# A chained accumulator read once at its third link, with the difference taken from SBUF

## Chip, cores and metric

One of the eight cores of a Trainium2 chip (trn2) runs the kernel. The metric is the device time of one execution in microseconds. The kernel before took 1004.42 us in the median of three runs (1003.59, 1004.42, 1004.70).

## What is computed

A gated recurrence over 6080 steps, two sequences, 256 channels, and then a feed-forward layer with 2048 hidden units and ELU. In float32:

```python
sig = 1.0 / (1.0 + np.exp(-f_logit))
f = lower_bound + (1.0 - lower_bound) * sig
for t in range(S):
    h = f[:, t] * h + (1.0 - f[:, t]) * x[:, t]
    y[:, t] = h
h = y.reshape(B * S, D) @ w_in
g = np.where(h > 0.0, h, np.exp(np.minimum(h, 0.0)) - 1.0)
out = g @ w_out
```

## The kernel before

Channels lie on the 128 partitions (two halves), time on the free axis. The sequence is cut into 12 pieces of 512 columns (one of 448); in each piece the 2048 hidden units are done in 8 steps ("quads", `quad`, line 924) of 2 x 128 units for both sequences. A quad multiplies the piece of y by a block of w_in (names M1 to M7, seven products in place of eight, after Strassen's scheme, into PSUM banks `hx`, `hv`, `hz`), applies ELU on ScalarE and VectorE (`elu`, tiles `e`, `g`, `hs`), splits the result into a rounded high part `gh` and a rest `gl` (`split`), and multiplies by a block of w_out, adding into four PSUM accumulators `o00`, `o01`, `o10`, `o11` (`second`, matmuls on line 797). Every product is made of three matmuls: high by high, high by low, low by high.

The work around the change: from the fourth piece on (number 3, counted from 0) the first quad of each piece is "wide": its second product too is done with seven products instead of eight. Four of them, P1, P6, P7 and P5 in this order (`wide_product`, line 838), go one after another into the same accumulator, `o11`, a chain: each link's running total is also a share of another output. So between the links `o11` is read out into the output tiles in SBUF (`out_tile`, traced as `v`): after P1 and P6 by ScalarE (k1, k2), after P7 twice: by ScalarE (k3, the copy of line 419, into the first sequence's output) and by VectorE (k4, subtracted from the second sequence's output); after P5 by VectorE again (k5, added to the same output). k4 and k5 both run through the helper of line 408 and read `v<-v,o`. There are nine wide quads, so nine of each. P5 may write `o11` only when every reader of the third link is done, and k3 and k4, which read the same bank, stand one after the other too.

The order of work on each engine is written by a planner before the program is built: `Plan.add` records every operation with an engine, a cost, a wanted time and what it reads and writes; `Plan.order` (line 223) simulates the engines with these costs and sorts all operations by the start it found; a table of shifts (`SHIFT`) moves single ones. Each engine then works through its own list in order, waiting on semaphores where an operation needs another engine's result.

Behind k5 on VectorE come, according to the piece, `q<-q,hz` (a sum over the bank `hz`, line 408), after which M2 may add into `hz`, or `g<-hv,e` (the ELU's last step, line 750), after which M7 may add into `hv`. Both M2 and M7 are matmuls of line 710.

Of the kernel before, what the change touches and what calls it, by code (L numbers as in the profile page):

```python
# [11 lines left out]
ALU = mybir.AluOpType  # L12
# [139 lines left out]
def wide(q):  # L152

    return q >= WIDE_FROM * MP and place(q)[1] < WIDE


def place(q):

    p, j = divmod(q, MP)
    return p, SECOND[j] if p == 1 else j  # L160


class Plan:
# [22 lines left out]

    def add(
        self, eng, cost, want, fn, reads=(), writes=(), adds=(), takes=(), lock=False, soonest=0.0,
        latest=None, other=None,
    ):  # L190

        i = len(self.ops)
        key = f"{self.key}.{self.count}"
        self.count += 1
        deps = set()
        for b in reads:
            w, r, a = self.last.setdefault(b, [set(), set(), set()])
            deps |= w | a  # L200
            r.add(i)
        for b in adds:
            w, r, a = self.last.setdefault(b, [set(), set(), set()])
            if r:
                self.last[b] = [set(), set(), {i}]
                deps |= w | r | a
                self.last[b][0] = set(w | r | a)
            else:
                deps |= w
                a.add(i)  # L210
        for b in writes:
            w, r, a = self.last.setdefault(b, [set(), set(), set()])
            deps |= w | r | a
            self.last[b] = [{i}, set(), set()]
        deps.discard(i)
        used = set(reads) | set(writes) | set(adds)
        self.ops.append(dict(
            eng=eng, cost=cost, want=want + SHIFT.get(key, 0.0), fn=fn, key=key, deps=deps, used=used, takes=list(takes),
            lock=lock, soonest=max(soonest + SHIFT.get(key + "@", 0.0), self.gate),
            latest=latest, other=other, patience=self.PATIENCE + SHIFT.get(key + "~", 0.0),  # L220
        ))

    def order(self):
        ops = self.ops
        n = len(ops)
# [40 lines left out]
        dropped = set()  # L266
        start = [0.0] * n
        done = [0.0] * n
        left = n
        while left:  # L270
            best = None
            for e, mine in waiting.items():
# [8 lines left out]
                for i in mine:  # L281
                    o = ops[i]
# [18 lines left out]
            t, _, i, _, e = best  # L301
            o = ops[i]
# [30 lines left out]
                        waiting[x].add(j)  # L333
        self.start, self.done = start, done
        assert not left
        return sorted(set(range(n)) - dropped, key=lambda i: (start[i], i))


def act_cost(n, ptr=False):
# [3 lines left out]
def dve_cost(n, fast=False):  # L343
    return 0.15 + n / (1920 if fast else 960)
# [11 lines left out]
def kernel(  # L356
# [7 lines left out]
    nc = tc.nc  # L364
# [8 lines left out]
    plan = Plan({**sizes, "h": 4, **{o: 1 for o in ("o00", "o01", "o10", "o11")}})  # L373
# [15 lines left out]
    def tl(kind, name, shape, dtype=F32):  # L389

        if name not in T:
            T[name] = pool[kind].tile(shape, dtype, tag=kind, name=kind)
        return T[name]
# [20 lines left out]
    def act(n, want, out_, in_, func=ACTF.Copy, ptr=None, **kw):  # L414
        args = {k: kw.pop(k) for k in ("scale", "bias") if k in kw}

        def fn():
            if func == ACTF.Copy:
                nc.scalar.copy(out=out_(), in_=in_())  # L419
            elif ptr:  # L420
                nc.scalar.activation(
                    out=out_(), in_=in_(), func=func, scale=ptr[0], bias=ptr[1]
                )
            else:
                nc.scalar.activation(out=out_(), in_=in_(), func=func, **args)  # L425

        plan.add("ACT", act_cost(n, ptr is not None), want, fn, **kw)
# [239 lines left out]
    def size(q):  # L667
        return SIZES[q // MP]
# [188 lines left out]
    def out_tile(p, t):  # L857
        return tl("v", ("out", p, t), [P, KD, SIZES[p]])

    def keep(p, e, t, want, op=None):  # L860

        o = ("out", p, t)
        reads = [("acc", p, 1, 1), o]
        if op is None:
            act(SIZES[p], want, lambda: out_tile(p, t)[:, e], lambda: accs[p, 1, 1],
                reads=reads, writes=[(o, e)], takes=[("v", o)])
        else:
            tt("DVE", SIZES[p], want, lambda: out_tile(p, t)[:, e], lambda: out_tile(p, t)[:, e],
               lambda: accs[p, 1, 1], op, psum=True, reads=reads, writes=[(o, e)],
               takes=[("v", o)])  # L870
# [53 lines left out]
    def quad(q):  # L924
        p, i = place(q)
        n = size(q)
        b = base(q)
        tail = q == NQ - 1
        w = wide(q)
        o = lambda name, value: plan.at(f"{stage(p)}{q % MP}.{name}", b + value)  # L930
        product = lambda name, bk, start, off: products(
            q, bk, [(LEFT[name], name)], start, o(name, off - 20))
        product("M1", "x", True, 0.0)
        product("M3", "v", True, 0.7)
        product("M4", "z", True, 1.4)
        qn = ("q", q)
        act(n, o("q", 0.9), lambda: tl("q", qn, [P, n]), lambda: hb(q, "x"), reads=[bank(q, "x")],
            writes=[qn], takes=[("q", qn)])
        for bk, off in (("v", 1.5), ("z", 2.2)):
            tt("DVE", n, o("q" + bk, off), lambda: T[qn], lambda: T[qn], lambda bk=bk: hb(q, bk),  # L940
               ALU.add, psum=True, reads=[bank(q, bk)], writes=[qn])
        product("M5", "v", False, 2.9)
        product("M2", "z", False, 4.8)
        g = ("g", q, 1)
        g1 = dict(name=g, tiles=[(1, 0), (0, 1)], pool="raw" if w else "g1", slots=4 if w else 2)
        elu(q, g1, 1, lambda: hb(q, "v"), [bank(q, "v")], o("e1", 3.7), True)
        elu(q, g1, 0, lambda: hb(q, "z"), [bank(q, "z")], o("e0", 5.6), True)
        product("M7", "v", False, 6.8)
        product("M6", "z", False, 8.8)
        if w:  # L950
            split(q, g, "DVE", o("s1", 8.2), (0,), ("b21", q))
            wide_product(q, 0, 0, 4 + 2, ("b21", q), 0, o("P2", 11))
        else:
            split(q, g, "DVE", o("s1", 8.2))
            second(q, g1, o("L1", 11))
        hs = ("hs", q)
        for j, (bk, off) in enumerate((("v", 7.6), ("z", 9.8))):
            tt("DVE", n, o("h" + bk, off), lambda j=j: tl("hs", hs, [P, 2, n])[:, j],
               lambda: T[qn], lambda bk=bk: hb(q, bk), ALU.subtract, psum=True,
               reads=[qn, bank(q, bk), hs], writes=[(hs, j)], takes=[("hs", hs)])  # L960
        g2 = dict(name=hs, tiles=[(0, 0), (1, 1)], pool="hs")
        elu(q, g2, None, lambda: T[hs].rearrange("p c n -> p (c n)"), [(hs, 0), (hs, 1)],
            o("e2", 10.9), False)
        if not w:
            split(q, hs, "DVE" if tail else "POOL", o("s2", 15))
            second(q, g2, o("L2", 18))
            return
        split(q, hs, "DVE", o("s2", 13))
        x, y = ("x", q), ("y", q)

        def xt():
            return T[g][:, 2:4]

        T_x = lambda: T.setdefault(x, xt())
        tt("DVE", 2 * n, o("X", 13.2), T_x, lambda: T[g][:, 1:2].to_broadcast([P, 2, n]),
           lambda: T[hs], ALU.subtract, reads=[g, (g, 1), hs, (hs, 0), (hs, 1)],
           writes=[(x, 0), (x, 1)])
        split(q, x, "DVE", o("sX", 14), hold=[g])
        tt("DVE", n, o("Y1", 15), lambda: T[hs][:, 1], lambda: T[hs][:, 1], lambda: xt()[:, 0],
           ALU.subtract, either=True, reads=[hs, g, (x, 0)], writes=[(hs, 1)])  # L980
        tt("DVE", n, o("Y0", 15.5), lambda: T[hs][:, 0], lambda: T[g][:, 0], lambda: T[hs][:, 1],
           ALU.subtract, either=True, reads=[g, (g, 0), hs, (hs, 1)], writes=[(hs, 0)])
        held = split(q, hs, "DVE", o("sY", 16), (0, 1), y, raw=YRAW)
        wide_product(q, 1, 1, 4 + 0, hs, 0, o("P1", 16))
        keep(p, 0, 0, o("k1", 17))
        wide_product(q, 0, 1, 2, hs, 1, o("P3", 17))
        wide_product(q, 1, 1, 1, y, 1, o("P6", 19), held)
        keep(p, 0, 1, o("k2", 20))
        wide_product(q, 1, 1, 3, x, 1, o("P7", 20))
        keep(p, 1, 0, o("k3", 21))  # L990
        keep(p, 0, 1, o("k4", 21), ALU.subtract)
        wide_product(q, 1, 1, 0, x, 0, o("P5", 21))
        keep(p, 0, 1, o("k5", 22), ALU.add)
        wide_product(q, 1, 0, 4 + 3, y, 0, o("P4", 21), held)
# [24 lines left out]
    for dst, a, b in ((fb, -0.5, 0.5), (fa, 0.5, 0.5)):  # L1019
# [3 lines left out]
                out=dst, in0=lb_sb, scalar1=a, scalar2=b, op0=ALU.mult, op1=ALU.add  # L1023
# [36 lines left out]
    for p in range(NP):  # L1060
        st = stage(p)
        if p:
# [5 lines left out]
            late = p > WIDE_FROM  # L1068
# [84 lines left out]
```

## Time and profile before

| | |
|---|---|
| median of three runs | 1004.42 us (1003.59 to 1004.70) |
| the profiled execution's own time | 1003.18 us |
| its span, first to last instruction | 1001.1 us |
| TensorE matmuls busy | 989.8 us (99%), 4338 |
| TensorE weight loads busy | 812.5 us (81%) |
| ScalarE busy | 806.9 us (81%) |
| VectorE busy | 786.5 us (79%) |
| GpSimd busy | 539.0 us (54%) |
| mean granted clock of TensorE | 0.998 |
| chain that ended last | 95% TensorE, 3% VectorE, 1% ScalarE |

PE stands for TensorE's matmuls, PEld for its weight loads (one ahead of each matmul, beside the matmul in front of it), DVE for VectorE, ACT for ScalarE, POOL for GpSimd. Busy matmuls overlap, so 99% doesn't mean that none can be late; a load that starts late is the sign of it.

### The profile page before, as it was taken

The page shows a single profiled execution, that of the slowest core. Times are in us where ns is not written, and L with a number is a line of the kernel's source. Part 1 is how long each engine was busy: PE and PEld are TensorE (multiplying, and loading weights), DVE is VectorE, ACT ScalarE, POOL GpSimd, SP SyncE. Part 2 cuts the span into 40 slices and gives each one's busy share as a digit, 9 for nine tenths or more (in the row PEclk, how much of TensorE's full clock was granted, in tenths as well). Part 3 has the DMA queues.
Part 4 walks back from the last instruction along what each step waited for, and adds up shares of the span by engine and source line. Part 5 has one row for each costly group of instructions (what it writes and reads, how often), then busy time and mean ns, then how long its engine had stood idle before and what let it go on. Part 6 is the DMA issues. An engine that isn't in the chain of part 4 may idle for free.

```text
span 1001.1 us, 11968 instructions
## 1 busy us (share of the span) xinstructions
PE 989.8 (99%) x4338; PEld 812.5 (81%) x4338; DVE 786.5 (79%) x958; ACT 806.9 (81%) x1137; POOL 539.0 (54%) x303
## 2 busy tenths in 40 slices
PE   7999999999999999999999999999999999999998
PEld 4788899888888878888888888888888888888886
DVE  7889788898888798778678678768767867877655
ACT  6888888977788789789788778888878978877864
POOL 0343647545548537654753862763765475376531
PEclk9999999999999999999999999999999999999999
DMA  5331202000030030021012003003002101200101
GB/s 210 127 121 37 97 31 84 36 1 1 1 127 1 1 126 1 1 85 43 1 53 74 1 1 127 1 1 127 1 0 84 43 1 49 78 1 0 43 1 43
DMA packets 9707, 46.51 MB, mean 46 GB/s; under 512 B 1200, under 2 KB 1200, under 8 KB 7088
## 3 DMA queue, kind: packets, MB, share of 16 engines
q1 hardware_dynamic: 9504, 45.75, 12.8%
q8 instruction: 34, 0.56, 0.2%
q14 instruction: 25, 0.20, 0.1%
q10 hardware_dynamic: 144, 0.00, 0.0%
HBM read 33.29 MB, written 12.45 MB: 46 GB/s over the span
## 4 chain that ended last, share of the span: by engine, by line
PE 95%; DVE 3%; ACT 1%; DMA 0%; issue 0%; DVEq 0%; ACTq 0%
PE o L797 50%; PE hz L710 17%; PE hv L710 17%; PE hx L710 6%; DVE y L638 1%; DMA raw<-w 0%; DVE v L408 0%; DVE gl L408 0%; PE h(_181 L695 0%; ACT e L425 0%; DVE e L750 0%; DVE raw L629 0%; DVE wiL L408 0%; DVE hs L750 0%; PE h(_267 L710 0%
## 5 line engine op out<-in xcount | busy, mean ns | idle before, releaser
L408 POOL TENSOR_TENSOR gl<-hs,gh 128x1024 fp32r<-128x1024 f32 (+1 forms) x79 | 199.2, 2526 | 195.3 <-ACT gh L419 187.6
L425 ACT ACTIVATE e<-e 128x512 f32<-128x512 f32 (+3 forms) x278 | 208.4, 757 | 6.6
L797 PE MATMUL o<-gh,woL 128*128 128x512 f32 (+1 forms) x706 | 212.5, 387 | 0.0
L797 PE MATMUL o<-gh,woH 128*128 128x512 f32 (+1 forms) x706 | 211.2, 387 | 0.1
L797 PE MATMUL o<-gl,woH 128*128 128x512 f32 (+1 forms) x706 | 208.6, 387 | 0.1
L710 PE MATMUL hz<-yo,wiH 128*128 128x512 f32 (+1 forms) x504 | 194.4, 390 | 0.3 <-DVE g L750 0.3
L710 PE MATMUL hv<-yo,wiH 128*128 128x512 f32 (+1 forms) x504 | 192.6, 388 | 0.0
L797 PEld LDWEIGHTS o<-gl,woH 128*128 128x128 f32 x706 | 132.4, 188 | 27.0 <-DVE gl L408 0.8
L797 PEld LDWEIGHTS o<-gh,woH 128*128 128x128 f32 x706 | 132.5, 188 | 26.8 <-ACT v L419 0.5
L797 PEld LDWEIGHTS o<-gh,woL 128*128 128x128 f32 x706 | 132.5, 188 | 26.4 <-ACT gh L419 0.2
L750 DVE SCALAR_TENSOR_TENSOR hs<-hs,e 128x1024 f32<-128x1024 f32 (+1 forms) x84 | 123.6, 1472 | 30.6 <-ACT e L425 30.5
L408 POOL TENSOR_TENSOR ys<-y 128x512 f32<-128x512 f32 (+1 forms) x52 | 95.0, 1830 | 70.8 <-DVE y L638 70.8
L419 ACT CAST gh<-hs 128x1024 fp32r<-128x1024 f32 (+1 forms) x95 | 98.7, 1039 | 35.2 <-PE o L797 17.2
L710 PEld LDWEIGHTS hz<-yo,wiH 128*128 128x128 f32 x504 | 94.6, 188 | 22.4 <-DVE q L408 2.3
L710 PEld LDWEIGHTS hv<-yo,wiH 128*128 128x128 f32 x504 | 94.6, 188 | 20.1 <-DVE g L750 0.2
L425 ACT ACTIVATE e<-hs 128x1024 f32<-128x1024 f32 (+1 forms) x84 | 88.3, 1051 | 26.6 <-DVE hs L408 19.6
L710 PE MATMUL hz<-yo,wiL 128*128 128x512 f32 (+1 forms) x252 | 97.9, 388 | 0.0
L710 PE MATMUL hv<-yo,wiL 128*128 128x512 f32 (+1 forms) x252 | 97.9, 388 | 0.0
L419 ACT CAST gh<-g 128x1024 fp32r<-128x1024 f32 (+1 forms) x80 | 83.1, 1039 | 15.0 <-PE o L797 10.0
L425 ACT ACTIVATE e<-hv 128x512 f32<-128x512 f32 (+1 forms) x84 | 49.8, 593 | 47.3 <-PE hv L710 29.4
L408 DVE TENSOR_TENSOR gl<-g,gh 128x1024 fp32r<-128x1024 f32 (+1 forms) x57 | 75.7, 1328 | 14.5 <-PE o L797 8.0
L408 POOL TENSOR_TENSOR gl<-g,gh 128x1024 fp32r<-128x1024 f32 (+1 forms) x23 | 57.4, 2496 | 54.6 <-PE o L797 36.3
(379 smaller groups left out, 1657.4 us busy)
## 6 DMA issues: line engine op xcount, KB each, us to landing
raw<-fx SPq DMA_DIRECT2D x20, 1024.0 KB, 4.9
out_t<-v SPq DMA_DIRECT2D x22, 512.0 KB, 2.7
raw<-w SPq DMA_DIRECT2D x16, 512.0 KB, 4.7
raw<-fx SPq DMA_DIRECT2D x2, 896.0 KB, 4.6
gh<-fx SPq DMA_DIRECT2D x2, 512.0 KB, 6.1
gl<-fx SPq DMA_DIRECT2D x2, 512.0 KB, 6.9
out_t<-v SPq DMA_DIRECT2D x2, 448.0 KB, 3.5
lb_sb<-lb ACTq DMA_DIRECT2D x1, 1.0 KB, 4.2
```

Of the source, the lines that this page charges most:

```text
L408: return e, cost, lambda: engines[e].tensor_tensor(out=out_(), in0=in0(), in1=in1(), op=op)
L419: nc.scalar.copy(out=out_(), in_=in_())
L425: nc.scalar.activation(out=out_(), in_=in_(), func=func, **args)
L638: nc.vector.tensor_tensor_scan(out=y4[:, a, :n], data0=f([k])[:, 0], data1=x([k])[:, 0], initial=init, op0=ALU.mult, op1=ALU.subtract,)
L710: nc.tensor.matmul(out=hb(q, b), lhsT=(wiH if m == "h" else wiL)[:, i, wi], rhs=T[kind, p, name], start=(start and j == 0), stop=(j == len ...
L750: lambda: nc.vector.scalar_tensor_tensor(out=gt(), in0=src(), scalar=0.0, in1=et(), op0=ALU.max, op1=ALU.subtract,), reads=src_names + [e] ...
L797: nc.tensor.matmul(out=accs[p, e, t], lhsT=lhsT, rhs=rhs, start=(c == 1), stop=(c == total(p, e, t)), skip_group_check=True,)
```

## The change

k4 no longer reads the accumulator. It subtracts k3's copy, which lies in SBUF (the first sequence's output tile), from the second sequence's output. In the planner it is recorded at the same place, with the same cost and the same reads as before, so that everything else is planned as it was; a new mark, `late`, then lifts it out of the finished list and puts it right behind the next VectorE operation that depends on it, which is k5. So the output first gets k5's sum and then the difference.

```diff
     def add(
         self, eng, cost, want, fn, reads=(), writes=(), adds=(), takes=(), lock=False, soonest=0.0,
-        latest=None, other=None,
+        latest=None, other=None, late=False,
     ):
...
         self.start, self.done = start, done
         assert not left
-        return sorted(set(range(n)) - dropped, key=lambda i: (start[i], i))
+        line = sorted(set(range(n)) - dropped, key=lambda i: (start[i], i))
+
+        for i in [i for i in line if ops[i]["late"]]:
+            k = next(k for k in range(line.index(i) + 1, len(line))
+                     if i in ops[line[k]]["deps"] and ops[line[k]]["eng"] == ops[i]["eng"])
+            line.insert(k, line.pop(line.index(i)))
+        return line
...
         keep(p, 1, 0, o("k3", 21))
-        keep(p, 0, 1, o("k4", 21), ALU.subtract)
+        o0, o1 = ("out", p, 0), ("out", p, 1)
+        plan.add(
+            "DVE", dve_cost(n), o("k4", 21), lambda: nc.vector.tensor_tensor(
+                out=out_tile(p, 1)[:, 0], in0=out_tile(p, 1)[:, 0], in1=out_tile(p, 0)[:, 1],
+                op=ALU.subtract,
+            ), reads=[("acc", p, 1, 1), o1], writes=[(o1, 0)], late=True,
+        )
         wide_product(q, 1, 1, 0, x, 0, o("P5", 21))
         keep(p, 0, 1, o("k5", 22), ALU.add)
```

The lists of PE, ACT, POOL and SP keep their order; on VectorE nine operations move by one to three places. VectorE in piece 6, before (k4 is the first row that reads `o_4612`, k5 the second):

```order
L408 TENSOR_TENSOR hs<-q,hz 128x512 [waits PE_49]
L408 TENSOR_TENSOR v<-v,o_4612 128x512 [waits DMAHW3_49,Activation_49]
L408 TENSOR_TENSOR hs<-q,hv 128x512 [waits PE_49]
L408 TENSOR_TENSOR v<-v,o_4612 128x512 [waits DVE_49,PE_49]
L408 TENSOR_TENSOR q<-q,hz 128x512 [waits PE_49]
L750 SCALAR_TENSOR_TENSOR hs<-hs,e_4706 128x1024 [waits DVE_49,Activation_49]
```

and the same place now (the six added lines of the planner shift the line numbers, 408 to 414 and 750 to 756; line 999 is the new subtraction):

```order
L414 TENSOR_TENSOR hs<-q,hz 128x512 [waits PE_49]
L414 TENSOR_TENSOR hs<-q,hv 128x512 [waits PE_49]
L414 TENSOR_TENSOR v<-v,o_4612 128x512 [waits DMAHW3_49,PE_49,Activation_49]
L999 TENSOR_TENSOR v<-v 128x512 [waits DVE_49,Activation_49]
L414 TENSOR_TENSOR q<-q,hz 128x512 [waits PE_49]
L756 SCALAR_TENSOR_TENSOR hs<-hs,e_4706 128x1024 [waits Activation_49]
```

`hs<-q,hv` moves ahead of k5, and the subtraction stands between k5 and `q<-q,hz`. Pieces 5 to 10 are alike; in pieces 3 and 4 `q<-q,hz` too moves ahead of k5, and the operation behind the subtraction is `g<-hv,e`. TensorE in the next piece that is alike, before (P5 is the three rows that write `o_5298` behind the products into `hv`):

```order
L710 MATMUL hv<-yo,wiH 128x512 x2
L710 MATMUL hv<-yo,wiL 128x512
L710 MATMUL hv<-yo,wiH 128x512
L797 MATMUL o_5298<-gh,wsH 128x512 [waits DVE_49]
L797 MATMUL o_5298<-gh,wsL 128x512
L797 MATMUL o_5298<-gl,wsH 128x512
```

and now:

```order
L716 MATMUL hv<-yo,wiH 128x512 x2
L716 MATMUL hv<-yo,wiL 128x512
L716 MATMUL hv<-yo,wiH 128x512
L803 MATMUL o_5298<-gh,wsH 128x512 [waits Activation_49]
L803 MATMUL o_5298<-gh,wsL 128x512
L803 MATMUL o_5298<-gl,wsH 128x512
```

Nothing moves; P5's first matmul waits for ScalarE (k3) in place of VectorE (k4). VectorE in the last piece, number 11, before:

```order
L408 TENSOR_TENSOR hs<-q,hv 128x512 [waits PE_49]
L408 TENSOR_TENSOR v<-v,o_8005 128x512 [waits DMAHW7_49,PE_49]
L408 TENSOR_TENSOR v<-v,o_8005 128x512 [waits DVE_49,PE_49]
L750 SCALAR_TENSOR_TENSOR hs<-hs,e_8137 128x1024 [waits Activation_49]
L750 SCALAR_TENSOR_TENSOR g_8171<-hv,e_8114 128x512 [waits Pool_49]
```

and now:

```order
L414 TENSOR_TENSOR hs<-q,hv 128x512 [waits PE_49]
L414 TENSOR_TENSOR v<-v,o_8005 128x512 [waits DMAHW7_49,PE_49]
L999 TENSOR_TENSOR v<-v 128x512 [waits DVE_49,Activation_49]
L756 SCALAR_TENSOR_TENSOR hs<-hs,e_8136 128x1024 [waits Activation_49]
L756 SCALAR_TENSOR_TENSOR g_8171<-hv,e_8114 128x512 [waits Pool_49]
```

Here k4 and k5 stood next to each other, and change places; the new second one reads SBUF alone and has the long `hs<-hs,e` (128x1024) and then `g<-hv,e` behind it.

## Rows read from the trace of the kernel before

**Rows 1.** The page's part 1: busy us (share of the span) xinstructions.

```profile
PE 989.8 (99%) x4338; PEld 812.5 (81%) x4338; DVE 786.5 (79%) x958; ACT 806.9 (81%) x1137; POOL 539.0 (54%) x303
```

**Rows 2.** Waits: engine line <- releaser: us in total, times, longest us.

```profile
PE h(_181 L695 <- DVE y L638: 4.0, 1, 4.0
...
PEld o L797 <- DVE v L408: 3.2, 7, 0.5
```

**Rows 3.** Timeline, piece 6: start us, us, engine line op out<-in [idle before <-releaser].

```profile
528.51 2.40 POOL L408 TENSOR_TENSOR gl<-hs,gh 128x1024 fp32r<-128x1024 f32 x1 [7.28 <-ACT gh L419]
...
528.74 0.59 ACT L419 COPY v<-o 128x512 f32<-128x512 f32 x1 [0.30 <-PE o L797]
...
529.37 0.69 DVE L408 TENSOR_TENSOR v<-v,o 128x512 f32<-128x512 f32 x1 [0.61 <-ACT v L419]
...
529.45 0.19 PEld L710 LDWEIGHTS hv<-yo,wiH 128*128 128x128 f32 x1
...
531.11 0.69 DVE L408 TENSOR_TENSOR v<-v,o 128x512 f32<-128x512 f32 x1 [0.46 <-PE o L797]
...
531.61 0.41 PEld L797 LDWEIGHTS o<-gl,woH 128*128 128x128 f32 x2
...
532.03 0.69 DVE L408 TENSOR_TENSOR q<-q,hz 128x512 f32<-128x512 f32 x1 [0.23 <-PE hz L710]
...
532.97 0.19 PEld L710 LDWEIGHTS hz<-yo,wiH 128*128 128x128 f32 x1
```

**Rows 4.** Timeline, piece 3, the first wide one.

```profile
287.83 0.19 PEld L797 LDWEIGHTS o<-gh,wsH 128*128 128x128 f32 x1 [0.29 <-ACT v L419]
...
289.44 0.68 DVE L750 SCALAR_TENSOR_TENSOR g<-hv,e 128x512 f32<-128x512 f32 x1
...
290.26 0.19 PEld L710 LDWEIGHTS hv<-yo,wiH 128*128 128x128 f32 x1
```

**Rows 5.** Timeline, piece 4.

```profile
368.42 0.68 DVE L408 TENSOR_TENSOR v<-v,o 128x512 f32<-128x512 f32 x1
...
369.01 0.69 DVE L750 SCALAR_TENSOR_TENSOR g<-hv,e 128x512 f32<-128x512 f32 x1
...
370.23 0.19 PEld L710 LDWEIGHTS hv<-yo,wiH 128*128 128x128 f32 x1
```

**Rows 6.** Timeline, VectorE, a pair in which the second reads the first's result.

```profile
294.28 1.22 DVE L629 SCALAR_TENSOR_TENSOR raw<-raw 128x1024 f32<-128x1024 f32 x1
295.53 1.28 DVE L638 TENSOR_TENSOR_SCAN y<-raw,y 128x512 f32<-128x512 f32 x1
```

**Rows 7.** The tile v: duration ns min/median/max, first and last start us, forms.

```profile
L408 DVE TENSOR_TENSOR v<-wiH,wiL x5: 677/684/1650, 95.0 to 234.5; 128x512 f32<-128x512 f32 x5
```

**Rows 8.** Timeline, 306 to 316 us, GpSimd and VectorE in turn.

```profile
308.93 1.52 DVE L638 TENSOR_TENSOR_SCAN y<-raw,y 128x512 f32<-128x512 f32 x1
...
309.33 3.32 POOL L408 TENSOR_TENSOR gl<-g,gh 128x1024 fp32r<-128x1024 f32 x1
...
310.38 3.37 DVE L750 SCALAR_TENSOR_TENSOR hs<-hs,e 128x1024 f32<-128x1024 f32 x1
```

**Rows 9.** Timeline, piece 11, the last.

```profile
939.59 0.19 PEld L797 LDWEIGHTS o<-gl,wsH 128*128 128x128 f32 x1 [0.23 <-ACT v L419]
...
940.24 2.41 POOL L408 TENSOR_TENSOR gl<-g,gh 128x1024 fp32r<-128x1024 f32 x1 [6.05 <-PE o L797]
...
940.59 0.69 DVE L408 TENSOR_TENSOR v<-v,o 128x512 f32<-128x512 f32 x1 [1.67 <-PE o L797]
...
941.63 2.10 DVE L750 SCALAR_TENSOR_TENSOR hs<-hs,e 128x1024 f32<-128x1024 f32 x1 [0.35 <-ACT e L425]
...
942.61 5.77 POOL L408 TENSOR_TENSOR gl<-hs,gh 128x1024 fp32r<-128x1024 f32 x2
...
944.72 0.19 PEld L710 LDWEIGHTS hv<-yo,wiH 128*128 128x128 f32 x1
```

**Rows 10.** Stretch 9.7:13.1: us, busy (x) of PE, PEld, DVE, ACT, POOL, PEclk, DMA, GB/s.

```profile
9.70:13.10 3.40, 3.27 (x5) 1.51 (x5) 3.33 (x4) 3.11 (x5) 0.00 (x0) 0.50 0.98 395
```

More of the change, by code (lines that the diff above doesn't have):

```diff
@@ L219, in add @@
             lock=lock, soonest=max(soonest + SHIFT.get(key + "@", 0.0), self.gate),
-            latest=latest, other=other, patience=self.PATIENCE + SHIFT.get(key + "~", 0.0),
+            latest=latest, other=other, late=late, patience=self.PATIENCE + SHIFT.get(key + "~", 0.0),
         ))
```

## Prediction

> **What bounds the kernel now.** I read the busy times first: TensorE has 4338 matmuls in 989.8 us of a span of 1001.1 us, 0.228 us from one to the next, and no other engine is over 81% [rows 1]. So time is won or lost only where TensorE is held back. Then the waits: the weight loads of line 797 waited seven times for VectorE's write of `v`, 3.2 us in all, 0.5 at most [rows 2]. The timeline of such a place (piece 6 of the sequence, [rows 3]) shows who is who. ScalarE's copy of the accumulator (k3) runs from 528.74 to 529.33; VectorE's subtraction (k4) follows at 529.37 and ends at 530.06. Both read `o11`, and P5, which writes it next, has to wait for the later one. Its first load would have stood one step (0.23) behind the load at 529.45, at 529.68, and VectorE let it go 0.38 later. From 529.45 to 531.61 there are eight steps in 2.16 us; at 0.228 each they would take 1.82. The stall therefore costs 0.34 (the 0.46 of idle that its row would show, less about 0.12 that the next loads make up; a load that is released x too late costs about x less 0.04). The profiled execution, 1003.18 us, lies 1.24 below the median of the three runs, 1004.42; I put every change onto the median.
>
> **What the change removes.** P5 now waits for k3 alone. k3 is over at 529.33, the load's place is 529.68: the wait vanishes with 0.35 to spare. That holds in the seven places of [rows 2], pieces 4 to 10: 7 x 0.34 = 2.38. In the first and the last wide piece k4 stood ahead of k3, so P5 waited for k3 behind it: 0.29 and 0.23 of idle [rows 4, 9], less 0.12 each, 0.28 together. There k3 will start straight behind P7. Sum removed: 2.66 us.
>
> **What it adds: the price of the new subtraction.** It has the same 512 columns, but both inputs are in SBUF now. The nearest rows, five sums of 512 columns with both inputs in SBUF, take 677 ns at least, 684 in the median and 1650 at most [rows 7]. I take 0.68 where GpSimd is idle, and look for GpSimd where it isn't. It reads what k5 has just written, so it cannot overlap k5's end: the scan that reads line 629's result starts 1.25 behind a start of 1.22 length, 0.03 after its end [rows 6], whereas an independent operation starts 0.59 behind one of 0.68 [rows 5]. So it starts 0.72 behind k5, and what follows it 0.60 later: where VectorE went from k5 to the next operation in 0.60, it now takes 1.32. The Trainium skill, VectorE: DVE Perf Modes, section The DRAIN you can't avoid, says that a semaphore between two VectorE operations costs nothing extra, since the next one never starts before the pipe is empty; by that the new one would start 0.60 behind k5 and eight of the terms below would shrink by 0.12 each, to a sum of about +0.3. The two rows above differ, so I go by them.
>
> **Who waits behind it.** One operation per piece stands behind the new subtraction and is awaited by TensorE.
> - Pieces 5 to 10 (six): `q<-q,hz`. k5 comes 0.32 earlier with P5, at 530.79, the subtraction at 531.51, `q<-q,hz` at 532.11, over at 532.80; before it was over at 532.72 [rows 3]. The load of `hz` that needs it stood at 532.97 and would now stand at 532.63: 0.17 late, 0.13 lost. Six times: 0.78. GpSimd's subtraction there ends at 530.91 [rows 3], before 531.51, so the SBUF operands cost nothing extra.
> - Piece 4: `g<-hv`. It stood 0.59 behind k5 at 369.01; now 368.42 - 0.33 + 1.32 = 369.41, over at 370.10. The load of `hv` stood at 370.23, now 369.89: 0.2 late, 0.16 lost [rows 5].
> - Piece 3, the first wide one: `g<-hv` at 289.44 [rows 4] becomes 289.44 - 0.16 + 0.72 = 290.00, over at 290.68. The load of `hv` at 290.26 would move to 290.08: 0.6 late, 0.55 lost.
> - Piece 11, the last: here GpSimd is in the way. Its subtraction runs from 940.24 to 942.65 and the next is queued right behind it (942.61, two in 5.77) [rows 9]. k5 is at 940.59, so the new operation comes up at about 941.2, in the middle of the first. VectorE's `hs<-hs,e`, two SBUF inputs, came up at 941.63 in the same place and took 2.10: it ended at 943.73, 1.08 after GpSimd's end [rows 9]. And whoever waits has the next turn: a scan ran from 308.93 to 310.45, a GpSimd operation issued at 309.33 meanwhile took 3.32, until 312.65, and VectorE's next one, issued at 310.38 right behind the scan, did not get in between but took 3.37, until 313.75, 1.1 after GpSimd's end [rows 8]. So in piece 11 the new subtraction gets its turn at about 942.5 and ends at 943.1; GpSimd's second, waiting since 942.5, goes next and takes 2.3, to 945.4; `hs<-hs,e` follows, 1.1 more, to 946.5; and `g<-hv` right behind it in the order is over at 947.1. The load of `hv` that needs it stood at 944.72 and would now stand at 944.61 [rows 9]. 2.45 late, about 2.4 lost, and nothing behind it can win that back on an engine that is 99% busy.
>
> The Trainium skill, SBUF — State Buffer, section Who interferes with whom, speaks against the change in the same way: a VectorE instruction with two SBUF inputs contends with a GpSimd instruction that reads SBUF, the earlier issue takes the shared pair for its whole length and the other stands still. By that rule GpSimd's second operation, queued at 942.5, goes ahead of a `hs<-hs,e` queued at 943.0, and rival 1 below would be out; the 3.37 above agrees.
>
> **Sum.** -2.66 + 0.78 + 0.16 + 0.55 + 2.4 = +1.2: **1005.6 us**. Nothing is costed for the final stores: they come tens of operations later and wait for the last products, not for k4.
>
> **Rivals.**
> 1. *VectorE keeps its turn in piece 11.* If `hs<-hs,e` goes straight behind the new subtraction, it ends about 0.5 later than before, `g<-hv` at 944.9, 0.3 late: 0.25 lost, not 2.4. Sum -0.9: 1003.5. For it: the two operations are next to each other in VectorE's queue, with no third engine's wait between. Against it: [rows 8], where the operation directly behind the scan lost its turn.
> 2. *Only the gain arrives.* If the subtraction overlaps k5's end and piece 3 and 11 have more slack than I read, -2.66: 1001.8. Against it: four different places where the operation behind k5 was already within 0.2 to 0.6 of being awaited.
> 3. *The stall in piece 11 takes the clock along* (slower). TensorE waited 4.0 us for the first `y` [rows 2], and the stretch behind it, 9.7 to 13.1, ran at a granted clock of 0.50, the 1.2 GHz level [rows 10]. If an idle of 2.4 us does the same, 3.4 us at half speed cost 1.7 more: +2.9, 1007.3. It decides only if the idle in piece 11 reaches its full length. Against it: 2.4 is well short of 4.0, and no idle of this length is in the trace.
> 4. *The middle pieces lose more* (slower). If the new subtraction takes 0.3 longer in each of the six, by a late k5 or by GpSimd, 6 x 0.3 = 1.8 more: 1007.4. The upper price of [rows 7] allows it; GpSimd's idle there speaks against it.
> 5. *It doesn't do what it says*: P5 still waits as long, now for ScalarE. Then the gain of 2.38 is missing: 1008. k3's end at 529.33, ahead of the load's place in the row, nearly excludes it.
>
> **How the numbers follow.** My forecast 55% (own range 1004.6 to 1006.8), rival 1 17%, rival 2 8%, rival 3 10%, rival 4 7%, rival 5 3%. A measurement of this kernel can tell about 0.2%, 2.0 us, from no change: 1002.4 to 1006.4 counts as the same. Rival 1 and nine tenths of the forecast lie in it, 0.65 with rounding; slower is rivals 3 to 5 and the forecast's upper end, 0.25; faster is rival 2 and a little of rival 1, 0.10. The range 1002.3 to 1007.4 leaves out rival 2, rival 5 and half of the outer ends.
>
> **What would show it.** In the profile after, the waits of line 797's loads for `v` should be gone but for traces. New ones should stand at `hz` for `q` (0.1 to 0.2, six times), at `hv` for `g` near 290 (0.6) and near 944 (2.4). The new line should appear nine times, about 0.7 us each, and once some 1.9 in the last piece, with a `hs<-hs,e` of some 3.5 us right behind it. If instead `hs<-hs,e` there stays near 2 us, rival 1 holds; if loads of P5 still wait, rival 5; a granted clock under 1.00 behind 944 is rival 3.

## Result, and the profile after

The changed kernel took **1010.22 us** in the median of five runs, 5.7 us above the 1004.53 of the kernel before on the same chip: ratio 1.0052, 95% interval 1.0036 to 1.0067. Run again later (e11 below) it took 1009.77, against 1005.28 of the kernel before on the same chip: 1.0040, interval 1.0028 to 1.0052. The forecast was 1005.6, at most 1007.4. The direction was right, the size was not: +1.2 foreseen, +5.7 and +4.5 measured.

The profiled execution took 1007.64 us, its span is 1005.5. Its busy times, to be held against [rows 1]:

```profile
PE 991.3 (99%) x4338; PEld 812.1 (81%) x4338; DVE 793.1 (79%) x958; ACT 806.6 (80%) x1137; POOL 539.0 (54%) x303
```

The same number of instructions on each engine, and VectorE 6.6 us busier: it stood in some of them and waited. The waits of TensorE's weight loads before, beside the row for `v` in [rows 2]:

```profile
PEld hz L710 <- DVE q L408: 2.3, 8, 0.4
...
PEld hz L710 <- DVE g L750: 1.1, 2, 0.7
...
PEld o L797 <- ACT v L419: 1.1, 3, 0.5
```

and after (408 is now 414, 419 is 425, 710 is 716, 750 is 756, 797 is 803):

```profile
PEld hv L716 <- DVE g L756: 5.0, 6, 2.5
...
PEld hz L716 <- DVE q L414: 4.7, 15, 0.4
...
PEld hz L716 <- DVE g L756: 2.2, 3, 1.0
...
PEld o L803 <- ACT v L425: 0.5, 1, 0.5
```

The seven waits for VectorE's `v` [rows 2] are gone, as foreseen, and of the three for ScalarE's `v` (k3) one is left. In their place `hz` waits for `q` seven times more, `hz` for `g` once more, now 1.0 at the longest, and `hv` waits for `g`, 2.5 us at its longest (before once, 0.2 us).

To see where the time went, take the start of each of the 4338 weight loads after, less the start of the same load before. This difference grows or shrinks only at these places:

```
place (us of before)         after less before    prediction
piece 3, 286 to 291          -0.16  +0.69         -0.17  +0.55
piece 3, 297 to 300                 +0.94                 0
piece 4, 366 to 371          -0.33  +0.23         -0.34  +0.16
pieces 5 to 10               -1.99  +1.64         -2.04  +0.78
piece 11, 938 to 946         -0.10  +2.41         -0.11  +2.4
650 to 653, 812 to 815              +1.17                 0
all else                            -0.06                 0
sum                                 +4.4                 +1.2
```

**Piece 11** is as foreseen. The timeline of VectorE and GpSimd after, to be held against [rows 9]:

```profile
942.60 0.69 DVE L414 TENSOR_TENSOR v<-v,o 128x512 f32<-128x512 f32 x1 [2.49 <-PE o L803]
943.39 1.83 DVE L999 TENSOR_TENSOR v<-v 128x512 f32<-128x512 f32 x1
945.15 3.41 DVE L756 SCALAR_TENSOR_TENSOR hs<-hs,e 128x1024 f32<-128x1024 f32 x1
948.48 0.68 DVE L756 SCALAR_TENSOR_TENSOR g<-hv,e 128x512 f32<-128x512 f32 x1
...
942.26 2.42 POOL L414 TENSOR_TENSOR gl<-g,gh 128x1024 fp32r<-128x1024 f32 x1 [5.97 <-PE o L803]
944.62 2.86 POOL L414 TENSOR_TENSOR gl<-hs,gh 128x1024 fp32r<-128x1024 f32 x1
...
949.21 0.19 PEld L716 LDWEIGHTS hv<-yo,wiH 128*128 128x128 f32 x1 [2.54 <-DVE g L756]
```

The new subtraction (line 999) comes up while GpSimd's first operation runs, and ends 0.54 behind it. GpSimd's second is waiting by then and goes next; `hs<-hs,e` ends 1.08 behind that, at 948.56. The load of `hv` stands 2.54.

**The middle pieces** lose twice what was foreseen. Piece 6 after, against [rows 3]:

```profile
532.00 0.69 DVE L414 TENSOR_TENSOR v<-v,o 128x512 f32<-128x512 f32 x1 [0.73 <-PE o L803]
532.80 0.69 DVE L999 TENSOR_TENSOR v<-v 128x512 f32<-128x512 f32 x1
533.41 0.68 DVE L414 TENSOR_TENSOR q<-q,hz 128x512 f32<-128x512 f32 x1
...
533.34 0.41 PEld L803 LDWEIGHTS o<-gh,woL 128*128 128x128 f32 x2
534.14 0.19 PEld L716 LDWEIGHTS hz<-yo,wiH 128*128 128x128 f32 x1 [0.39 <-DVE q L414]
```

From k5 to the new subtraction it is 0.79, not 0.72. The load of `hz` had its place two steps behind 533.34, at 533.80, and stands at 534.14: 0.34 late, not 0.17.

**Piece 3** has a second loss that was not foreseen. After:

```profile
288.68 0.69 DVE L414 TENSOR_TENSOR v<-v,o 128x512 f32<-128x512 f32 x1 [1.72 <-ACT raw L431]
289.47 0.69 DVE L999 TENSOR_TENSOR v<-v 128x512 f32<-128x512 f32 x1
...
291.53 1.97 DVE L756 SCALAR_TENSOR_TENSOR hs<-hs,e 128x1024 f32<-128x1024 f32 x1 [0.77 <-ACT e L431]
...
295.27 3.31 DVE L644 TENSOR_TENSOR_SCAN y<-raw,y 128x512 f32<-128x512 f32 x1
...
289.53 2.89 POOL L414 TENSOR_TENSOR gl<-hs,gh 128x1024 fp32r<-128x1024 f32 x1 [1.88 <-ACT gh L425]
295.08 2.42 POOL L414 TENSOR_TENSOR gl<-hs,gh 128x1024 fp32r<-128x1024 f32 x1 [2.66 <-ACT gh L425]
...
299.22 0.19 PEld L716 LDWEIGHTS hz<-yo,wiH 128*128 128x128 f32 x1 [1.03 <-DVE g L756]
```

Before, the scan started at 295.53 and took 1.28 [rows 6], ahead of this row of GpSimd:

```profile
295.83 3.20 POOL L408 TENSOR_TENSOR gl<-hs,gh 128x1024 fp32r<-128x1024 f32 x1 [3.15 <-ACT gh L419]
```

Now GpSimd's subtraction is 0.19 ahead of it, and the scan takes 3.31. `g<-hz` behind it is late, and the load of `hz` stands 1.03. The lines also show GpSimd's operation before that one: it comes up at 289.53, 0.06 behind the new subtraction, and takes 2.89, and `hs<-hs,e` ends 1.08 behind its end. VectorE itself had waited 0.77 for ScalarE ahead of `hs<-hs,e`. What follows from that is read below, beside the run that has the subtraction further back.

### The profile page after: what moved, and what is told of

Read it like the earlier page. It is cut to its first block, busy times and chain, and to the rows that moved or that the text cites. A ratio compares the mean times of both kernels' runs of the same rounds, so it can differ in the third digit from the quotient of the medians.

```text
span 1005.5 us, 11962 instructions
## 1 busy us (share of the span) xinstructions
PE 991.3 (99%) x4338; PEld 812.1 (81%) x4338; DVE 793.1 (79%) x958; ACT 806.6 (80%) x1137; POOL 539.0 (54%) x303
## 4 chain that ended last, share of the span: by engine, by line
PE 92%; DVE 5%; ACT 2%; issue 1%; DMA 0%; DVEq 0%; ACTq 0%
PE o L803 48%; PE hz L716 16%; PE hv L716 16%; PE hx L716 5%; DVE y L644 1%; DVE gl L414 1%; ACT e L431 1%; DVE hs L756 1%; DVE q L414 0%; DMA raw<-w 0%; DVE g L756 0%; DVE v L414 0%; DVE raw L635 0%; PE h(_181 L701 0%; DVE e L756 0%
## 5 line engine op out<-in xcount | busy, mean ns | idle before, releaser
L414 DVE TENSOR_TENSOR gl<-g,gh 128x1024 fp32r<-128x1024 f32 (+1 forms) x57 | 78.4, 1376 | 14.5 <-PE o L803 8.0
L414 POOL TENSOR_TENSOR yo<-ys,yo 128x512 fp32r<-128x512 f32 (+1 forms) x51 | 75.7, 1489 | 25.0 <-ACT yo L425 19.1
```

Of the source, the lines that this page charges most:

```text
L414: return e, cost, lambda: engines[e].tensor_tensor(out=out_(), in0=in0(), in1=in1(), op=op)
```

## Experiments

The twelve runs, e1 to e12, start from the changed kernel; e11 is the changed kernel itself. The others have a table, `BEHIND`, of the pieces that get the new subtraction and its place: 1 is directly behind k5, as in the change, 2 is one VectorE operation further back, and so on. A piece that is not in the table keeps the old k4, which reads PSUM ahead of P5.

```diff
+            for _ in range(ops[i]["late"] - 1):
+                k = next(j for j in range(k + 1, len(line)) if ops[line[j]]["eng"] == "DVE")
             line.insert(k, line.pop(line.index(i)))
...
+        if p in BEHIND:
...
-                ), reads=[("acc", p, 1, 1), o1], writes=[(o1, 0)], late=True,
+                ), reads=[("acc", p, 1, 1), o1], writes=[(o1, 0)], late=BEHIND[p],
...
+        else:
+            keep(p, 0, 1, o("k4", 21), ALU.subtract)
```

In their rows, e11 aside, the new subtraction is line 1003, and the other lines lie 3 higher than after the change (414 is 417, 716 is 719, 756 is 759). Differences are of medians against the kernel before on the same chip, with the 95% interval of the ratio in us.

### The change without piece 11, in piece 11 alone, in piece 3 alone, and one place further back

```diff
+BEHIND = {3: 1, 4: 1, 5: 1, 6: 1, 7: 1, 8: 1, 9: 1, 10: 1}
```

> The change in pieces 3 to 10, the old subtraction (from PSUM, ahead of the last link) in piece 11. Theory A (piece 11 alone costs 2.4 us, by the turn that GpSimd takes in the shared pair, and the stall of TensorE there takes the granted clock down for some us, 2.7 us more in most runs): 1010.2 - 2.3 - 2.7 = about 1005.2 us, granted clock 0.998 in every run. Theory B (the clock falls elsewhere, as behind piece 3's stall of 1.03 us at the load of hv or hz): about 1007.9 us, clock 0.995 in most runs. Theory C (piece 11 costs nothing in the unprofiled runs): about 1010 us.

```diff
+BEHIND = {11: 1}
```

> The change in piece 11 alone, the old subtraction in pieces 3 to 10. Theory A: 1004.5 + 2.3 + 2.7 = about 1009.5 us, granted clock 0.995 in most runs. Theory B (the clock falls elsewhere): 1004.5 + 2.3 = about 1006.8 us, clock 0.998 in every run.

```diff
+BEHIND = {3: 1}
```

> The change in piece 3 alone. Theory A (piece 3 loses 0.55 at the load of hv and 0.94 at the load of hz because GpSimd takes its turn ahead of the scan): 1004.5 + 1.5 = about 1006.0 us, clock 0.998. If the second loss is chance and not bound to the change: about 1005.0 us. If the clock falls here (theory B): about 1008.7 us with clock 0.995.

```diff
+BEHIND = {4: 2, 5: 2, 6: 2, 7: 2, 8: 2, 9: 2, 10: 2}
```

> Pieces 4 to 10: the new subtraction stands one VectorE operation further back, behind the one that TensorE waits for next (q<-q,hz, in piece 4 g<-hv); the old subtraction in pieces 3 and 11. If the loss in these pieces is only the place ahead of the awaited operation: the 0.3 us of each piece is kept, 7 x 0.33 = 2.3 us, about 1002.2 us (0.6 us more for each turn of the shared pair that happens to fall the other way). Rival (the 0.6 us is only handed on to hs<-hs,e and from there to the next loads): 0.25 us given back in each piece, about 1004.0 us.

Measured: without piece 11 1005.81, **+0.7** (0.2 to 2.0). Piece 11 alone 1008.42, **+3.3** (1.9 to 4.2). Piece 3 alone 1006.10, **+1.0** (0.3 to 2.0), with the same 0.69 and 0.94 in its trace as the change. One place further back 1002.66, **-2.4** (-3.5 to -1.6).

So piece 11 is the largest part, and its median lies above the 2.3 us that its wait explains, though the interval takes them in. The trace of the run with piece 11 alone shows what can come on top. TensorE's wait for `hv`, and then the windows of the trace (us, busy and number for PE, PEld, DVE, ACT and POOL, granted clock, DMA, GB/s):

```profile
948.54 0.50 PE L719 MATMUL hv<-yo,wiH 128*128 128x512 f32 x1 [2.11 <-DVE g L759]
```

```profile
945.00:949.00 4.00, 1.89 (x9) 1.27 (x8) 4.00 (x3) 1.03 (x1) 1.80 (x1) 1.00 0.00 0
949.00:951.00 2.00, 2.00 (x7) 1.55 (x6) 1.90 (x4) 0.02 (x1) 1.90 (x1) 0.52 0.00 0
951.00:953.00 2.00, 2.00 (x8) 1.55 (x7) 0.76 (x2) 0.60 (x2) 0.47 (x1) 0.63 0.00 0
953.00:955.00 2.00, 2.00 (x10) 1.68 (x9) 0.00 (x0) 1.97 (x3) 0.00 (x0) 1.00 0.00 0
```

Behind an idle of 2.11 us the clock is at half, the 1.2 GHz level, for about 3.4 us. The loads there fall back by 3.9 us (the 0.1 gained at P5 taken off) where the change's own trace has 2.3: 1.6 us are the clock's. That was rival 3, with its price of 1.7. It does not come every time: after the change, in both of its traces, an idle of 2.12 us stood at the same place and the clock stayed at 1.00. Of the four traces with this stall (the change, the change again, piece 11 alone, e12) two show the fall.

The expectation for the clock named the mean over a whole run as the sign. That sign was badly chosen: this mean runs from 0.995 to 1.000 in the runs of the kernel before too, because the start of the program varies ([rows 10] shows its half clock; in the traces of e2 and e3 that stretch ran at 1.00). Only the windows tell.

The one place further back keeps the whole gain of the middle pieces, 2.4 us at the loads. (In its trace an input that landed late held ScalarE for 1.65 us in piece 6 and cost 0.74 there; the traces of e5 and e9 with the same order have no such step.) Piece 6 in this order, from the trace of e9 below:

```profile
529.75 0.69 DVE L417 TENSOR_TENSOR v<-v,o 128x512 f32<-128x512 f32 x1 [0.73 <-PE o L806]
530.60 0.69 DVE L417 TENSOR_TENSOR q<-q,hz 128x512 f32<-128x512 f32 x1 [0.16 <-PE hz L719]
531.21 0.68 DVE L1003 TENSOR_TENSOR v<-v 128x512 f32<-128x512 f32 x1
532.32 1.23 DVE L759 SCALAR_TENSOR_TENSOR hs<-hs,e 128x1024 f32<-128x1024 f32 x1 [0.43 <-ACT e L434]
```

`q<-q,hz` again waits for TensorE and not the other way round, and the subtraction lies in time that VectorE spends waiting for ScalarE. In pieces 4 and 10 VectorE has no such idle there, and the next operation starts 0.60 behind the subtraction; still the loads show no loss in any of the seven. Nothing is handed on to TensorE.

### Piece 11: the place, or the operand; piece 3: which of its neighbours

```diff
+BEHIND = {4: 2, 5: 2, 6: 2, 7: 2, 8: 2, 9: 2, 10: 2, 11: 8}
```

> As the run with pieces 4 to 10 one operation further back, and in piece 11 too the new subtraction, seven VectorE operations behind the second sum, where both VectorE and GpSimd are idle for over 2 us; the old one in piece 3. If what costs in piece 11 is the pair shared with GpSimd at one moment: nothing is lost there, 0.1 us is gained, about 1002.4 us (2.5 below before), and TensorE's load of hv in piece 11 has no wait over 0.5 us. If the earlier start of the last link costs by itself in piece 11: about 1005 us or more.

```diff
+BEHIND = {11: 1}
...
-                out=out_tile(p, 1)[:, 0], in0=out_tile(p, 1)[:, 0], in1=out_tile(p, 0)[:, 1],
+                out=out_tile(p, 1)[:, 0], in0=out_tile(p, 1)[:, 0], in1=accs[p, 1, 1],
```

> In piece 11 alone the subtraction stands directly behind the second sum, as in the change, but reads the accumulator in PSUM (after the last link, so that it computes something else) and not the copy in SBUF; pieces 3 to 10 as before. If the operand in SBUF is what costs in piece 11 (the subtraction then waits for GpSimd's read and GpSimd gets the next turn ahead of hs<-hs,e): the subtraction takes 0.7 us, hs<-hs,e still gets its turn, and the kernel stands within 0.5 us of before, about 1005 us. If the place ahead of hs<-hs,e is what costs: 2.3 us more than before at least, 1007.4 to 1009 us.

```diff
+BEHIND = {3: 13}
```

> In piece 3 alone the new subtraction, twelve VectorE operations behind the second sum (about 15 us later); pieces 4 to 11 as before. If both losses of piece 3 (0.55 at hv, 0.94 at hz) come from the subtraction's place on VectorE: 0.16 to 0.3 us gained, about 1004.8 us. If the second loss comes from ScalarE and GpSimd, which are no longer held behind the old subtraction and take their turn ahead of the scan: 0.94 - 0.2 = 0.7 us lost, about 1005.8 us, and the scan takes over 3 us again.

```diff
+BEHIND = {3: 2}
```

> In piece 3 alone the new subtraction one VectorE operation further back, behind g<-hv that TensorE waits for; pieces 4 to 11 as before. It then asks for the pair while GpSimd reads (289.5 to 291.9 us in the changed kernel) and holds up hs<-hs,e. If turns decide: hv is no longer late (0.55 us saved), but hs<-hs,e starts at about 292.5 us instead of 291.5, and the scan behind it loses its turn: about 1006 us. If the place ahead of g<-hv was the whole loss: about 1004.8 us.

Measured: eighth place in piece 11, 1001.60, **-2.0** (-3.0 to -1.3), with no wait of `hv` in piece 11. From PSUM 1004.48, **+0.9** (-0.3 to 1.6). Piece 3 at place 13, 1003.33, **-0.3** (-1.3 to 0.5); at place 2, 1005.44, **+1.8** (0.9 to 2.6).

The run from PSUM has the subtraction at the very place of the change, with one operand exchanged:

```profile
941.62 0.69 DVE L417 TENSOR_TENSOR v<-v,o 128x512 f32<-128x512 f32 x1 [2.49 <-PE o L806]
942.34 0.69 DVE L1003 TENSOR_TENSOR v<-v,o 128x512 f32<-128x512 f32 x1
942.95 1.81 DVE L759 SCALAR_TENSOR_TENSOR hs<-hs,e 128x1024 f32<-128x1024 f32 x1
...
941.28 2.40 POOL L417 TENSOR_TENSOR gl<-g,gh 128x1024 fp32r<-128x1024 f32 x1 [5.98 <-PE o L806]
943.63 5.75 POOL L417 TENSOR_TENSOR gl<-hs,gh 128x1024 fp32r<-128x1024 f32 x2
```

It takes 0.69 beside the same GpSimd operation that held it for 1.83, and `hs<-hs,e` keeps its turn. The load differences show no loss at `hv`, only 0.42 ahead of it, where the next chain into `o11` waited for this extra reader. So the operand costs the 2.4 us, not the place alone. With both inputs in SBUF the place then decides whom it meets.

In piece 3, place 13:

```profile
291.49 1.48 DVE L759 SCALAR_TENSOR_TENSOR hs<-hs,e 128x1024 f32<-128x1024 f32 x1 [1.57 <-ACT e L434]
...
294.73 1.28 DVE L647 TENSOR_TENSOR_SCAN y<-raw,y 128x512 f32<-128x512 f32 x1
...
289.48 2.41 POOL L417 TENSOR_TENSOR gl<-hs,gh 128x1024 fp32r<-128x1024 f32 x1 [1.86 <-ACT gh L428]
295.03 3.20 POOL L417 TENSOR_TENSOR gl<-hs,gh 128x1024 fp32r<-128x1024 f32 x1 [3.15 <-ACT gh L428]
```

and place 2:

```profile
290.82 2.61 DVE L1003 TENSOR_TENSOR v<-v 128x512 f32<-128x512 f32 x1
293.35 1.21 DVE L759 SCALAR_TENSOR_TENSOR hs<-hs,e 128x1024 f32<-128x1024 f32 x1
...
296.33 3.31 DVE L647 TENSOR_TENSOR_SCAN y<-raw,y 128x512 f32<-128x512 f32 x1
...
290.46 2.43 POOL L417 TENSOR_TENSOR gl<-hs,gh 128x1024 fp32r<-128x1024 f32 x1 [1.87 <-ACT gh L428]
296.01 2.55 POOL L417 TENSOR_TENSOR gl<-hs,gh 128x1024 fp32r<-128x1024 f32 x1 [3.12 <-ACT gh L428]
```

With the subtraction out of the way the scan is again 0.30 ahead of GpSimd, though ScalarE and GpSimd start as early as in the change. So the second loss is the subtraction's too: my guess that the freed ScalarE by itself lets GpSimd overtake is refuted. The way it takes is through GpSimd. `hs<-hs,e` starts no later in the change than here (291.53 and 291.49), since it waits for ScalarE both times. But in the change GpSimd's `gl<-hs,gh`, 0.06 behind the new subtraction, takes 2.89 in place of 2.41; `hs<-hs,e` ends 1.08 behind GpSimd's end both times, so it takes 1.97 in place of 1.48. That puts the scan about 0.5 later, and it had 0.30 to spare. The earlier start of k3 has its part: it brought GpSimd's operation from 290.27 in the kernel before to 289.53, beside the subtraction. At place 2 `hv` is on time, as expected, but the subtraction now comes up behind GpSimd's first operation, takes 2.61 and holds up `hs<-hs,e` itself; the scan comes 0.32 behind GpSimd's second, and 1.78 are lost at `hz`, more than the 0.69 and 0.94 together.

### All places chosen; the middle alone; the change again; place 2 in piece 11

```diff
+BEHIND = {3: 13, 4: 2, 5: 2, 6: 2, 7: 2, 8: 2, 9: 2, 10: 2, 11: 8}
```

> The new subtraction in all nine pieces, each where no awaited operation stands behind it and GpSimd does not hold the pair for long: twelve operations behind the second sum in piece 3, one in pieces 4 to 10, seven in piece 11. If the gains add up: 0.16 + 2.32 + 0.10 = 2.6 us below before, and faster than the change by 7 us or so. If earlier loads only make later turns fall the other way (0.59 each): 1.5 to 2 us below before.

```diff
+BEHIND = {4: 1, 5: 1, 6: 1, 7: 1, 8: 1, 9: 1, 10: 1}
```

> Pieces 4 to 10 alone as in the change, the subtraction directly behind the second sum; pieces 3 and 11 as before. By the prediction's own terms: 7 x 0.34 - 0.16 - 6 x 0.13 = 1.4 us below before. By the trace of the changed kernel, where 0.24 to 0.31 us are given back in each piece: 2.3 - 1.8 = 0.5 us below before.

> The change itself, on one chip with the three others. By the sum of the parts run alone (piece 3 +1.0 to 1.5, pieces 4 to 10 -0.5, piece 11 +2.3, and +1.6 more where the granted clock falls to half behind the stall): 3 to 5 us above before, about 4 in the middle.

```diff
+BEHIND = {11: 2}
```

> In piece 11 alone the new subtraction one operation further back, behind hs<-hs,e and ahead of g<-hv that TensorE waits for; pieces 3 to 10 as before. If turns of the pair decide: hs<-hs,e keeps its turn, GpSimd's next read is already waiting and comes next (about 2.4 us), the subtraction waits for it, and g<-hv starts at about 945.6 us instead of 943.7, so the load of hv is late by 1.8 us or so: 1.8 us above before, 3.4 where the clock falls too. If the first awaited operation alone matters: about 0.5 us above before.

Measured: chosen places 1002.67, **-2.6** (-3.7 to -1.7). The middle alone 1005.05, **-0.2** (-1.3 to 0.5). The change again 1009.77, **+4.5** (2.8 to 5.2). Place 2 in piece 11 1008.39, **+3.1** (1.8 to 4.2).

The chosen places add up to what the parts gave, against both other kernels: the ratio to before is 0.9973 (0.9963 to 0.9983), and on the same chip the change stood 7.1 us higher. Its profiled execution took 1000.32 us; the loads gain 0.16, 2.4 and 0.10 in pieces 3, 4 to 10 and 11 and lose nothing there. The new subtraction is the same nine operations, 0.69 in the median, and even its 1.48 beside GpSimd is free there, because VectorE then waits another 1.57 us for ScalarE:

```profile
L1003 DVE TENSOR_TENSOR v<-v x9: 681/686/1482, 302.2 to 944.5; 128x512 f32<-128x512 f32 x9
```

Place 2 in piece 11 shows that "one further" is no rule:

```profile
942.36 2.54 DVE L759 SCALAR_TENSOR_TENSOR hs<-hs,e 128x1024 f32<-128x1024 f32 x1
944.83 2.87 DVE L1003 TENSOR_TENSOR v<-v 128x512 f32<-128x512 f32 x1
947.62 0.68 DVE L759 SCALAR_TENSOR_TENSOR g<-hv,e 128x512 f32<-128x512 f32 x1
...
943.79 3.36 POOL L417 TENSOR_TENSOR gl<-hs,gh 128x1024 fp32r<-128x1024 f32 x1
```

`hs<-hs,e` keeps its turn, but GpSimd's next operation waits behind it and has the following one; that one ends at 947.15, the subtraction 0.55 behind it, and `hv` waits 2.52 us, as long as in the change. The load differences give 4.0 us lost there, 1.6 of it the clock's by the account above, with the clock at 0.50 in the stretch 949 to 951. I had expected 1.8 without the clock, since I took GpSimd's end from the wrong start: it starts its read only when `hs<-hs,e` is over.

## Why the prediction was wrong

**What held.** P5's wait is gone, and the gain of 2.66 stands in the trace as 2.6 (0.16, 0.33, 1.99, 0.10). P5's release by k3 held: rival 5 is out. Piece 11's 2.4 came as 2.41, by the mechanism that was written down: the subtraction 1.83 long (some 1.9 foreseen), `hs<-hs,e` 3.41 (some 3.5). Rival 1 is out. The Trainium skill's rule (SBUF — State Buffer, Who interferes with whom), that two SBUF inputs on VectorE and a read by GpSimd exclude each other, is borne out by the run from PSUM: 0.69 against 1.83 at one place.

**Step that failed 1: "One operation per piece stands behind the new subtraction and is awaited by TensorE", in piece 3.** The price at `g<-hv` was about right (0.55 foreseen, 0.69 measured). But the sum ended there, and the prediction's "I take 0.68 where GpSimd is idle, and look for GpSimd where it isn't" was not carried through in this piece: nothing in it asks where GpSimd will be once k3 is earlier, or what the subtraction does to GpSimd. GpSimd's operation came up 0.06 behind the subtraction and was 0.48 longer; `hs<-hs,e`, which stood beside it, 0.49 longer; and the scan had only 0.30 to spare on GpSimd, by [rows 6] and GpSimd's row at 295.83. It lost its turn: 0.94 more. Place 13 shows that without the subtraction there is no such loss, and place 2 that it comes again when the subtraction delays `hs<-hs,e` directly.

**Step that failed 2: "0.17 late, 0.13 lost. Six times: 0.78".** It was 0.24 to 0.31 each, 1.64 together, with piece 4's 0.23 against 0.16. Three small durations were too short at once: 0.79 from k5 to the subtraction and not 0.72, 0.05 from the end of `q<-q,hz` to the load that it releases, taken as nothing, and some 0.05 at k5 itself. Together 0.17, on a lateness of 0.17. The 0.72, with 0.03 behind an end from the scan of [rows 6], is right for the run from PSUM (941.62 to 942.34, with the same dependence on k5); with both inputs in SBUF every one of the nine pairs leaves 0.10. So the extra 0.07 goes with the operand in SBUF (nine pairs against one); why, no run shows. With that the middle pieces gain next to nothing: -1.4 by the terms, -0.5 in the trace, -0.2 (-1.3 to 0.5) in the run alone. The Trainium skill's rule against this term (VectorE: DVE Perf Modes, The DRAIN you can't avoid) would have made it smaller still; the rows say 0.79 for the dependent operation and 0.61 for the independent one behind it.

**Step that failed 3: "Against it: 2.4 is well short of 4.0", rival 3 at 10%.** The clock did fall behind the stall in two traces of four, 1.6 us each time. A single row with a 4.0 us idle says nothing of how short an idle may be.

**The sum by the runs.** Piece 3 +1.5 and the middle -0.45 by the loads, piece 11 +2.3: 3.3 without the clock, 4.9 with it. Measured 4.5 and 5.7, with intervals from 2.8 to 6.7. The parts run alone give +1.0, -0.2 and +3.3, together +4.1. Two parts are open: in what share of the unprofiled runs the clock falls, and whether the steps of 0.6 of the last section, two of them in the profiled execution, come more often with the change.

## What to carry to other kernels

An operation that is moved off TensorE's path should be put behind the next operation that TensorE awaits, at a place where its engine waits for another anyway: the same nine operations cost 4.5 us at one place and save 2.6 at another. Before an operand is moved from PSUM to SBUF on VectorE, look at what GpSimd does at that moment, and then at who has the next turn: the loss is not the wait of the operation itself (1.1 us in piece 11) but GpSimd's whole next operation ahead of the one that counts. It goes the other way too: such an operation holds GpSimd, and what VectorE does beside GpSimd next is late by that (0.5 us in piece 3), though VectorE itself had idle time between. So follow the delay on both engines past the first awaited operation, to every place where VectorE is only some tenths ahead of GpSimd.

## What the runs showed of the hardware

**Two operations that come up within 0.01 us of each other take the turn either way.** In pieces 4 to 9 VectorE's `gl<-g,gh` and GpSimd's `ys<-y` come up together. Before:

```profile
648.93 1.22 DVE L408 TENSOR_TENSOR gl<-g,gh 128x1024 fp32r<-128x1024 f32 x1
...
648.94 2.37 POOL L408 TENSOR_TENSOR ys<-y 128x512 f32<-128x512 f32 x1
```

and after:

```profile
650.02 2.37 DVE L414 TENSOR_TENSOR gl<-g,gh 128x1024 fp32r<-128x1024 f32 x1
...
650.03 1.28 POOL L414 TENSOR_TENSOR ys<-y 128x512 f32<-128x512 f32 x1
```

The starts lie 0.01 apart both times, and the turn falls differently; TensorE loses about 0.6 when GpSimd has it (once 0.9). In the fourteen traces the two starts lie 0.01 apart or less at all 84 such places, and GpSimd has the turn at 18 of them: none in the trace before, two after the change and three in its second trace. The same gap goes both ways, so a single turn looks like chance, and I take it for one source of the spread of the kernel before (1003.45 to 1006.87 in 26 runs); no run was made to show that. One trace alone would have booked 1.17 us to the change. Whether the change makes such turns more frequent stays open: they are 9 of 24 in the four traces with the subtraction directly behind k5 in the middle pieces, 4 of 18 in the three with it one place further back, and 5 of 42 in the seven with the old order there. If that difference were real, it would be about 0.9 us of the change (an estimate: 6 places, 9/24 less 5/42, 0.6 us each).

**The clock can fall behind an idle of 2.1 us, and need not.** 2.11 and 2.10 us of idle (piece 11 alone, e12) were followed by half clock, 2.12 in the two traces of the change was not. What decides between them stays open.
